# DeltaNet and GELU-MLP on one core: the norms' epsilon on Pool, one query mask by ScalarE and Pool, the last outputs from two queues, and a new order

## The chip, the cores and the metric

The kernel runs on one core of one Trainium2 chip. The time is the device time of one execution in microseconds, 270.38 us as the median of three runs. The engines are PE (TensorE, with its weight loads shown as PEld), DVE (VectorE), ACT (ScalarE), Pool (GpSimd) and SP (SyncE, which here only issues DMAs). Each engine works through its own queue in order and waits on semaphores for the others.

## The reference

`q`, `k` and `v` are (4, 8, 768, 48) and `beta` is (4, 8, 768), all f32. A delta rule runs over the 768 positions of each of the 32 heads, and a two-layer network with a GELU follows:

```python
k_n = k / (np.linalg.norm(k, axis=-1, keepdims=True) + 1e-06)
for t in range(S):
    y[:, :, t] = q[:, :, t] @ state                      # per head, state is 48 x 48
    v_old = k_n[:, :, t] @ state
    state = state + beta[:, :, t] * outer(k_n[:, :, t], v[:, :, t] - v_old)
x = y.transpose(0, 2, 1, 3).reshape(3072, 384)
h = x @ w_in                                             # 384 x 2048
g = 0.5 * h * (1 + tanh(sqrt(2 / pi) * (h + 0.044715 * h**3)))
out = g @ w_out                                          # 2048 x 384
```

The output is (3072, 384) in f32.

## The kernel before

The 768 positions are cut into 12 chunks of 64. A chunk has two units of eight head pairs each, so there are 24 units; unit `u` belongs to chunk `u // 2`. In each unit, 128 partitions hold two heads' 64 positions.

For each chunk, SP loads `k`, `q` and `v` (`k3.01` is one of four loads of chunk 3's keys). The norms are a short chain: `sq` (squares), `sum` (DVE), `pow` (the root; on ACT for the first two chunks, by a power on Pool after that), `eps` (adds 1e-6), `inv` (reciprocal) and `ib` (times minus beta). Chunk 0 is done in two halves, `0a` and `0b`. Minus beta comes from `betaT` (PE transposes) and `betaN` (eight small DVE copies).

For each unit, `kn` and `kb` scale the keys and `qb` converts the queries; `Tk`/`Tq` or `T` transpose them on PE and `kTk`/`kTq`/`kT` copy the result, or `turn` transposes by DMA. Products of keys with keys and queries (`GM` and `GQ` for units 0 to 3, `G2` and `G` for the rest) are copied through a triangular mask by DVE: `ln`, `wpm`, `wpq` or `wp`. A triangular system is then solved in five steps. `X1` sets up a block-diagonal tile `bd`; in step i a product `A` and a DVE addition `rt` (or, as an alternative, products `J` and `C` and a plain copy `rj`) give the right side of a product `B`, and B goes back into `bd`: either in two copies from PSUM (`bde`, ACT or DVE), or in one copy from PSUM (`xi`, ACT or DVE) and two from SBUF (`bdc`, Pool or DVE).

For each chunk, `K`, `R`, `U`, `Un`, `S`, `Sn` carry the state from chunk to chunk (`Sn` is the new state), and `Q`, `O`, `On` give the output `y`. `X` and `xT` transpose it on PE with a copy, or `turnx` by DMA. The network follows: 16 `up` groups of three matmuls, four `gelu` on ACT, eight `down` groups of four matmuls, two copies `Z` to SBUF, and the stores `out`. The `fill` operations are PE products of zeros.

What runs when is written out in one text, `ORDER`: a list of all operations with the engine behind a colon (`a` ACT, `d` DVE, `g` Pool, `s` SP) and the PSUM bank behind `@`. Each engine's queue is the list's operations on that engine, in the list's order. `Flow.add` names an operation with the engines that it may have, and what it reads and writes; `Flow.order` reads the text; `Flow.emit` works out the semaphore waits from the operations' reads and writes. Of two alternatives (`alt`), only the one named in the text runs.

The lines that the profile names: L333 is the helper `copy` (all plain copies); L416 the loads; L438 and L439 `sq`; L440 `sum`; L441 and L442 `pow`; L444 `eps`; L446 `inv`; L447 `ib`; L464 and L466 `kn` and `kb`; L475 `Tk`, `Tq`, `T`; L488 `turn`; L499 the products of keys and queries; L503 the masks; L529 and L531 `X1`; L540 `A`, `B`, `C`; L550 `rt`; L575 `bdc`; L397 and L402 `betaT` and `betaN`; L664 `X`; L681 `up`; L692 `down`; L701 and L704 the stores.

Of the kernel before, what the change touches and what calls it, by code (L numbers as in the profile page):

```python
# [29 lines left out]
Tq.1@0 fill37@6 J4.1@7 A5.0@3 fill19@6 X11.2:d ln.3 X10.2:d X11.3:d kTq.1:d wpm.3 w2.0 w2.1 C4.1 rj4.1:a sq.2:a bdz5:g X10.3:g R0b.0:g  # L30
A1.2@1 R0a.0:d rt5.0 C1.3 B4.1@0 bde40.1:a bde41.1:a GQ.1@6 B5.0@3 Tq.0@4 fill56@5 A5.1@0 rj1.3:d rt1.2 B1.2@5 rt5.1 sum.2 B5.1@2 kTq.0:d
wpq.1 fill65@0 B1.3@1 fill59@0 xi5.0:a bde11.2:a bde10.2:a bde50.1:a bde11.3:a bdc50.0:g bdc51.0:g qb.3:a bde51.1:a fill5@3 A2.2@0 bde10.3:d
A2.3@1 Tq.3@6 fill2@7 fill49@3 fill69@7 fill38@3 kTq.3:a rt2.2 rt2.3 B2.3@7 B2.2@6 bde20.2:a pow.2 eps.2 inv.2 bde20.3:d bde21.3:a bde21.2:d
U.0@2 GQ.0@0 GQ.3@4 Un.0:a A3.2@6 A3.3@7 qb.2:a wpq.0 rt3.3 O.0@2 fill6@0 B3.3@7 Tq.2@0 On.0:a X.0@1 wpq.3 rt3.2 xi3.3:a triwpm5:a S.0@2
fill28@7 kTq.2:d xT.0:d bdc31.3:d Sn.0:d B3.2@0 bde30.2:d bdc30.3:d kn.4:g ib.2:g kb.5:g bdz4:g kb.4:g kn.5:g sq.3:g qb.4:a qb.5:a bde31.2:a
ladj32.3:a up0.0@6 up1.0 up2.0 T.4@4 kT.4:d up3.0 up12.0@0 A4.2@2 A4.3@3 ladj16.3:d rt4.3 up13.0 G2.4@4 ladj16.2:a gelu0.0 up14.0 B4.3@3
rt4.2 ln.4 K.1@6 xi4.3:a up15.0 up4.0@4 up5.0 gelu3.0 R.1 bdc41.3:d sum.3 bdc40.3:g X10.4:g X11.4:g G.4@2 wp.4 B4.2@6 up8.0@0 up6.0 up7.0
up9.0 A5.3@7 up10.0 turn.5 q3.00 q3.01 q3.10 q3.11 k5.11 q4.00 k4.10 k5.00 k4.00 k5.10 q4.11 k4.01 k4.11 bde41.2:a bde40.2:a gelu1.0 rt5.3
A1.4@2 A5.2@3 GQ.2@6 G2.5@4 up11.0 rt1.4 rt5.2 wpq.2 B1.4@2 down10.0@3 pow.3 eps.3 inv.3 kn.6:g ln.5 kn.7:d ib.3:g kb.7:g X11.5:g X10.5:g
kb.6:g down11.0 B5.3@6 gelu2.0 bde11.4:a bde10.4:a G.5@0 Q.1@4 A2.4@2 B5.2@7 down12.0 down13.0 wp.5 rt2.4 bde50.2:d B2.4@2 down00.0@0  # L40
bde51.3:a qb.6:a qb.7:a bde51.2:a bde50.3:a A1.5@1 bde21.4:a rt1.5 U.1@6 turn.7 turn.6 k5.01 q6.11 bde20.4:a Un.1:a down01.0 B1.5@1 down02.0
O.1 A3.4@2 sq.4:d sum.4 pow.4 bde11.5:a bde10.5:a A2.5@1 down03.0 On.1:a Z1.0:a Z0.0:a rt3.4 rt2.5 X.1@4 B3.4@5 G2.7@2 bde31.4:a bde30.4:a
xT.1:d G.7@0 S.1@6 ln.7 Sn.1 B2.5@4 up8.1@2 A4.4@5 up9.1 bde20.5:a bde21.5:a sq.5:a eps.4 rt4.4 G2.6@6 up10.1 B4.4@5 A3.5@4 up11.1 ln.6
# [222 lines left out]
def bass_deltanet__then__act_gelu_tanh_kernel(  # L266
# [20 lines left out]
    A = F.add  # L287

    with nc.allow_non_contiguous_dma("strided loads"), nc.allow_low_precision("bf16 pipeline"):
# [39 lines left out]
        def hf(a, n=C):  # L329
            return slice(64 * a, 64 * a + n)  # L330

        def copy(e, out, in_):
            return e.activation(out, in_, ACT.Copy) if e is nc.scalar else e.tensor_copy(out, in_)  # L333

        PE, SP, EV = ("pe",), ("sp",), ("act", "dve")
        quad = [(p, a) for a in range(2) for p in range(2)]

# [418 lines left out]
```

## Time and profile before

| | |
|---|---|
| median of 3 runs (270.02 to 271.37) | 270.38 us |
| the profiled execution | 269.08 us |
| its span, first to last instruction | 267.4 us |
| mean granted TensorE clock | 0.997 |
| ACT busy | 191.3 us (72%) |
| Pool busy | 128.5 us (48%) |

The span is what the profile shows of the program; the execution's own time has 1.7 us more around it. The shares are of busy time, and for PE they say only that some matmul was under way. Sequencer work (waits, branches and issuing DMAs) does not count as busy. In a row of the timeline the first number is the start and the second the length, in microseconds from the start of the span.

### The profile page before, as it was taken

To read this page: it belongs to the slowest core of one execution; us is meant where nothing else is said; L and a number is where in the kernel's file an instruction comes from. 1 tells how busy PE (TensorE), PEld (TensorE's weight loads), DVE (VectorE), ACT (ScalarE), POOL (GpSimd) and SP (SyncE) were. 2 spreads that over 40 slices of the span, in tenths; PEclk is the share of its full clock that TensorE was granted. 3 is DMA by queue.
4 is the path that set the end of the run, shared out by engine and by line. 5 is a ranking of instruction groups with operands and counts; after the bars stand their busy time and mean duration, and the time that the engine had idled before them with its cause. 6 is when DMAs were issued, how large, how long until landed. Compare 5 with 4: busy or idle time off the path is not lost.

```text
span 267.4 us, 12235 instructions
## 1 busy us (share of the span) xinstructions
PE 242.7 (91%) x5476; PEld 188.9 (71%) x5484; DVE 212.3 (79%) x367; ACT 191.3 (72%) x298; POOL 128.5 (48%) x176
## 2 busy tenths in 40 slices
PE   1489768998999999999999999999999999999994
PEld 0266457776877787886877986976878868778672
DVE  4689999997899998898789987997898587786200
ACT  5646798689898878895887887784777837736450
POOL 5746556485788746671816532983652321011000
PEclk9999999999999999999999999999999999999998
DMA  4899997859889979899785979587515510331023
GB/s 79 143 169 187 163 193 122 151 109 141 170 144 159 145 136 169 160 153 133 158 166 92 178 136 133 103 173 130 87 44 100 99 32 2 93 61 29 5 60 88
DMA packets 119540, 32.05 MB, mean 120 GB/s; under 512 B 113600, under 2 KB 118720, under 8 KB 119488
## 3 DMA queue, kind: packets, MB, share of 16 engines
q1 hardware_dynamic: 115248, 27.88, 60.5%
q0 software_dynamic: 2880, 3.15, 7.4%
q8 instruction: 43, 0.70, 1.1%
q10 hardware_dynamic: 1360, 0.25, 0.5%
q14 instruction: 9, 0.07, 0.1%
HBM read 20.64 MB, written 4.72 MB: 95 GB/s over the span
## 4 chain that ended last, share of the span: by engine, by line
PE 55%; DVE 13%; ACT 11%; SPq 7%; DMA 6%; issue 2%; POOL 2%; ACTq 1%; DVEq 0%
PE ps L681 18%; PE ps L692 15%; PE ps L540 13%; SPq L416 6%; ACT bd L333 5%; DMA kT<-tok 4%; PE ps L499 3%; ACT gT L685 2%; DVE rt L550 2%; PE ps L606 2%; DVE bd L531 1%; DVE wp L503 1%; PE ps L652 1%; DVE bd L333 1%; DMA kraw<-in_k_dram 1%
## 5 line engine op out<-in xcount | busy, mean ns | idle before, releaser
L333 ACT ACTIVATE bd<-ps 64x512 bf16<-64x512 f32 x142 | 82.4, 589 | 23.6 <-PE ps L540 21.1
L681 PE MATMUL ps<-xT,W 128*128 128x256 bf16 x576 | 76.5, 273 | 0.6 <-ACT bd L333 0.4
L692 PE MATMUL ps<-W,gT 128*128 128x384 bf16 x384 | 73.3, 326 | 0.0
L685 ACT ACTIVATE gT<-ps 128x1024 bf16<-128x1024 f32 x48 | 48.4, 1020 | 13.9 <-PE ps L681 13.5
L681 PEld LDWEIGHTS ps<-xT,W 128*128 128x128 bf16 x576 | 50.5, 98 | 7.2 <-ACT bd L333 0.6
L550 DVE TENSOR_TENSOR rt<-ps,two 128x512 bf16<-128x512 f32 x67 | 45.2, 683 | 8.0 <-PE ps L540 7.5
L575 POOL COPY bd<-xi 64x256 f32<-64x256 f32 x39 | 16.5, 422 | 67.5 <-ACT xi L333 53.4
L692 PEld LDWEIGHTS ps<-W,gT 128*128 128x128 bf16 x384 | 33.1, 98 | 17.0 <-ACT gT L685 0.2
L529 POOL TENSOR_SCALAR_AFFINE_SELECT bd<-ln 64x512 bf16<-64x512 bf16 x35 | 23.1, 662 | 19.8 <-DVE ln L503 17.1
L442 POOL TENSOR_TENSOR nrm<-nrm,half 128x16 f32<-128x16 f32 x10 | 29.4, 2944 | 4.8 <-DVE nrm L440 4.1
L503 DVE CAST_PREDICATED wp<-mup,ps 128x1024 bf16<-128x1024 uint16 (+1 forms) x28 | 29.8, 1063 | 0.3
L540 PE MATMUL ps<-wp,bd 128*128 128x64 bf16 (+1 forms) x576 | 26.8, 188 | 3.2 <-ACT xi L333 0.9
L540 PE MATMUL ps<-rt,bd 128*128 128x64 bf16 x576 | 28.3, 194 | 0.9 <-DVE rt L550 0.7
L550 DVE TENSOR_TENSOR rl<-ps,two 128x256 bf16<-128x256 f32 (+1 forms) x47 | 22.4, 485 | 8.0 <-PE ps L540 7.7
L540 PEld LDWEIGHTS ps<-wp,bd 128*128 128x128 bf16 x576 | 22.7, 98 | 7.9 <-ACT bd L333 1.4
L333 DVE CAST bd<-ps 64x512 bf16<-64x512 f32 x38 | 25.9, 684 | 2.9 <-PE ps L540 2.3
L540 PEld LDWEIGHTS ps<-rt,bd 128*128 128x128 bf16 x576 | 23.5, 98 | 5.2 <-DVE rt L550 1.1
L540 PE MATMUL ps<-ln,bd 128*128 128x64 bf16 (+1 forms) x384 | 18.0, 188 | 2.8 <-DVE bd L333 1.6
L540 PEld LDWEIGHTS ps<-ln,bd 128*128 128x128 bf16 x384 | 14.9, 97 | 7.7 <-ACT bd L333 3.0
L503 DVE CAST_PREDICATED ln<-mlo,ps 128x512 bf16<-128x512 uint16 x24 | 16.4, 683 | 4.7 <-PE ps L499 4.4
L466 POOL TENSOR_TENSOR tok<-kraw,nrm 128x384 bf16<-128x384 f32 x22 | 18.1, 826 | 3.9 <-PE ps L639 3.3
L540 PE MATMUL ps<-rl,bd 128*128 128x64 bf16 x384 | 19.0, 193 | 0.7 <-DVE rl L550 0.7
(95 smaller groups left out, 324.0 us busy)
## 6 DMA issues: line engine op xcount, KB each, us to landing
qraw<-in_q_dram SPq DMA_DIRECT2D x48, 96.0 KB, 3.4
vraw<-in_v_dram SPq DMA_DIRECT2D x48, 96.0 KB, 3.5
kraw<-in_k_dram SPq DMA_DIRECT2D x44, 96.0 KB, 3.2
out_dram<-ob SPq DMA_DIRECT2D x22, 192.0 KB, 3.1
W<-in_moe_w_in_dram POOLq DMA_DIRECT2D x2, 768.0 KB, 10.4
W<-in_moe_w_out_dram POOLq DMA_DIRECT2D x2, 768.0 KB, 11.4
out_dram<-ob SPq DMA_DIRECT2D x4, 96.0 KB, 2.2
kT<-tok SPq DMA_TRANSPOSE x19, 4.6
```

The lines of the kernel that those rows point to most:

```text
L333: return e.activation(out, in_, ACT.Copy) if e is nc.scalar else e.tensor_copy(out, in_)
L416: lambda e, P, n=n, a=a, y=y, xs=xs, view=view: e.dma_start(raw[n][s][hf(a), :, :].rearrange("p (xg y) d -> p xg y d", y=2)[:, xs, y, :], ...
L442: if e is nc.scalar else e.tensor_tensor(nr[:, 1, hx], nr[:, 0, hx], half[:, hx], ALU.pow), reads=[nrn, "half"] + ["one"] * (c < ROOTS),
L466: A(("dve", "pool"), op("kb"), lambda e, P: e.tensor_tensor(kb, kr, nr[:, 4, hx].unsqueeze(2).to_broadcast(full), ALU.mult), reads=[f"kraw ...
L503: return e.copy_predicated(out.rearrange("p (x g) t -> p x g t", x=2), mask[:, 0:wd].bitcast(U16).unsqueeze(1).unsqueeze(1).to_broadcast([ ...
L529: A(("pool", "dve"), op(f"X1{a}"), lambda e, P, src=ln[m][hf(a), :, :], dst=bd[b_][hf(a), :, hf(a)], a=a: e.affine_select(out=dst, in_=src ...
L540: ins = e.matmul(P(name)[:, C * h + lo:C * h + C], bd[b_][:, h, :], rhs[:, h, lo:C], **kw)
L550: A(("dve",), op(f"rt{i}"), lambda e, P, i=i, lo=lo, r_=r_: e.tensor_tensor(r_[:, :, lo:C], P(ps(f"A{i}")).rearrange("p (h t) -> p h t", h ...
L575: A(("pool", "dve"), op(f"bdc{i}{a}"), lambda e, P, src=xi[i_][hf(a), :, :], dst=bd[b_][hf(a), :, hf(a)]: e.tensor_copy(dst.bitcast(F32), ...
L681: ins = e.matmul(P(ph)[:, 256 * f:256 * f + 256].rearrange("p (x t) -> p x t", x=2), W1[:, j, 128 * (i + f):128 * (i + f) + 128], x_[:, :, ...
L685: A(("act",), f"gelu{i // 4}.{c}", lambda e, P, i=i, ph=ph: e.activation(g_[:, i:i + 4, :], P(ph).rearrange("p (f t) -> p f t", f=4), ACT. ...
L692: ins = e.matmul(P(po)[:, 0:DM], g_[:, f, 128 * b:128 * b + 128], W2[:, f, :], start=(f == 0), stop=(f == FC - 1))
```

## The change

Four edits to what an operation may do, and a new `ORDER` for all of them:

- `eps` may run on Pool. In the new order 10 of the 13 do, each behind its `pow` in Pool's queue.
- The query mask of units 0 to 3 gets an alternative: `wqa`, a copy by ACT out of PSUM, and `wqb`, a product with the mask by Pool in SBUF, in place. The new order uses it for unit 1.
- The last chunk's four stores may be issued from SP or ACT, each with its own semaphore. In the new order `out01.11`, `out00.11` and `out10.11` are SP's and `out11.11` is ACT's.
- `betaN` goes through a helper `neg`, which knows ACT too; the engines allowed stay DVE alone.

```diff
+        def neg(e, out, in_):
+            return e.activation(out, in_, ACT.Copy, scale=-1.0) if e is nc.scalar else e.tensor_scalar(out, in_, -1.0, None, op0=ALU.mult)
...
-                A(("dve",), f"eps.{z}", lambda e, P, nr=nr, hx=hx: e.tensor_scalar(nr[:, 2, hx], nr[:, 1, hx], 1e-6, None, op0=ALU.add),
+                A(("dve", "pool"), f"eps.{z}", lambda e, P, nr=nr, hx=hx: e.tensor_scalar(nr[:, 2, hx], nr[:, 1, hx], 1e-6, None, op0=ALU.add),
...
+                A(("act",), op("wqa"), lambda e, P: copy(e, wp[s][:, :, C:2 * C].rearrange("p (x g) t -> p x g t", x=2), P(ps("GQ")).rearrange(
+                    "p (x r) -> p x r", x=2)[:, :, 0:4 * C].rearrange("p x (g t) -> p x g t", g=4)), frees=[ps("GQ")], writes=[n("wpq")], alt=(op("wq"), 1))
+                A(("pool",), op("wqb"), lambda e, P: e.tensor_tensor(wp[s][:, :, C:2 * C], wp[s][:, :, C:2 * C], mup[:, 0:C].unsqueeze(1).to_broadcast([128, H, C]), ALU.mult),
+                  reads=["mup"], writes=[n("wpq")], alt=(op("wq"), 1))
...
-                        A(SP, f"out{b}{a}.{c}", lambda e, P, a=a, b=b, r0=r0, o_=o_: e.dma_start(out[r0:r0 + C, :], o_[hf(a), b, :]), reads=[f"{on}.{b}"],
-                          dma=f"o{c % 2}")
+                        A(("sp", "act"), f"out{b}{a}.{c}", lambda e, P, a=a, b=b, r0=r0, o_=o_: e.dma_start(out[r0:r0 + C, :], o_[hf(a), b, :]),
+                          reads=[f"{on}.{b}"], dma=f"oz{b}{a}")
```

In the new order the counts of some operations on their engines differ as well (before, after):

| | DVE | ACT | Pool |
|---|---|---|---|
| `bde` | 38, 50 | 142, 132 | |
| `xi` | 6, 12 | 24, 17 | |
| `bdc` | 21, 16 | | 39, 42 |
| `X1` | 13, 9 | | 35, 39 |
| `eps` | 13, 3 | | 0, 10 |
| `qb` | 3, 2 | 12, 4 | 9, 18 |
| `sq` | 1, 1 | 5, 8 | 7, 4 |
| `xT` | 3, 0 | 1, 6 | |
| all | 367, 368 | 295, 274 | 168, 190 |

PE has 692 operations before and 689 after: 34 `fill` instead of 38, six `X` instead of four (chunks 7, 8 and 10 are turned by PE in place of DMA, chunk 6 by DMA in place of PE), and one `J` fewer. The text's beginning and end, before:

```
one:d tmplz:d tmpl0 tmpl1 pad1:d wz:g fill8@0 k0x0.00:a k0x0.01:a k0x0.10:s k0x0.11:s k0x1.10:a triln3:a k0x1.00:a half:d bdz1:d bdz3:d
...
down12.11 down13.11 down00.11@5 down01.11 down02.11 down03.11 out00.9 Z1.11:d out11.11 out10.11 out00.10 Z0.11:a out01.11 out00.11
```

and after, where ACT's queue begins with `k0x0.10 k0x0.11 k0x1.10 k0x1.11 k0x1.01 beta00 ladj16.3 two sq.0a tabS ladj32.0 pow.0a pow.0b` and the last words are

```
down02.11 down03.11 out00.10 Z0.11:d out01.11:s out00.11:s down12.11 down13.11 Z1.11:a out11.11:a out10.11:s
```

## The prediction

> **What bounds the kernel now.** I read the page's head first: the span, and each engine's busy time.
>
> ```profile
> span 267.4 us, 12235 instructions
> ...
> PE 242.7 (91%) x5476; PEld 188.9 (71%) x5484; DVE 212.3 (79%) x367; ACT 191.3 (72%) x298; POOL 128.5 (48%) x176
> ```
>
> PE is busy for 91% of the span, yet DVE and ACT are at 79% and 72%, and an average over the whole span hides which of them sets the pace where. So next came busy time by stage. I cut the stages at marks that exist in both orders: 17.6 us is where DVE starts `ln.1` (the second unit's first mask), 49.7 where it ends `kT.4` (chunk 2's first keys), 147.1 where it ends `rt4.13`, 241.2 where it ends `rt4.23` (the last unit's fourth step).
>
> ```profile
> 0.00:17.60 17.60, 7.73 (x105) 5.01 (x107) 10.90 (x38) 9.93 (x18) 10.81 (x26) 1.00 0.71 121
> ...
> 17.60:49.70 32.10, 25.97 (x555) 18.74 (x561) 30.05 (x53) 24.59 (x42) 18.39 (x22) 1.00 1.06 166
> 49.70:147.10 97.40, 93.81 (x2322) 73.92 (x2323) 86.91 (x140) 79.88 (x126) 61.09 (x70) 1.00 0.86 146
> 147.10:241.20 94.10, 92.79 (x2229) 74.81 (x2226) 78.48 (x130) 65.56 (x99) 37.70 (x57) 1.00 0.54 98
> 241.20:267.40 26.20, 22.36 (x274) 16.48 (x272) 5.99 (x11) 11.33 (x14) 0.52 (x1) 0.97 0.19 44
> ```
>
> The first number behind a window is its length; then come PE, PEld, DVE, ACT and POOL busy, each with its instructions. The opening is a start-up: PE has 7.73 of 17.6 us. From 17.6 to 49.7 DVE is full (30.05 of 32.1, 94%) while PE has 81%: DVE sets the pace. From 49.7 to 147.1 PE has 96% and DVE 89%: PE is the bound, and its gaps are opened by the engines that feed it. From 147.1 to 241.2 PE has 99% and DVE 83%: PE alone. The rest is PE's last feed-forward work and the outputs. So the span is a start-up, a stage paced by DVE, then PE's work plus its gaps, then a tail. A change of order is worth what it does to these four.
>
> The prices of the work that changes hands most, from the groups by line with shapes kept apart (busy, then mean ns of one, then idle time before):
>
> ```profile
> L333 ACT ACTIVATE bd<-ps 64x512 bf16<-64x512 f32 x142 | 82.4, 589 | 23.6 <-PE ps L540 21.1
> ...
> L333 DVE CAST bd<-ps 64x512 bf16<-64x512 f32 x38 | 25.9, 684 | 2.9 <-PE ps L540 2.3
> ...
> L333 DVE CAST xi<-ps 128x512 bf16<-128x512 f32 x6 | 4.1, 687 | 0.6 <-PE ps L540 0.5
> ...
> L575 DVE COPY bd<-xi 64x256 f32<-64x256 f32 x21 | 7.5, 359 | 1.4 <-ACT xi L333 0.9
> ...
> L444 DVE TENSOR_SCALAR nrm<-nrm 128x16 f32<-128x16 f32 x11 | 3.1, 286 | 0.5 <-POOL nrm L442 0.4
> ```
>
> **The change, part by part.** I counted the operations of both orders by name and engine and priced each by the mean of its own shape's group. Over the kernel DVE gets 12 more of the `bde` copies at 684 ns (+8.2) and 6 more `xi` (+4.1 at 687 ns), and gives away 10 epsilons (-2.9 at 286 ns), 5 `bdc` (-1.8 at 359 ns) and smaller things: all its operations come to 227.1 us before and 231.1 after. ACT loses 10 `bde` at 589 ns (-5.9) and others: 196.6 to 186.1. Pool gets 127.2 to 135.6. What counts is where these fall.
>
> *Start-up.* These rows of the timeline (start, length) are the chain from the first loads to the second unit's mask.
>
> ```profile
> 0.82 2.04 ACTq L416 DMA_DIRECT2D kraw<-in_k_dram  x3
> ...
> 2.89 1.28 ACT L333 ACT_TABLE_LOAD   x1 [2.89 <-issue]
> ...
> 4.72 0.51 ACT L438 ACTIVATE sq<-kraw 128x384 f32<-128x384 f32 x1
> ...
> 7.29 0.21 ACT L441 ACTIVATE nrm<-nrm 128x8 f32<-128x8 f32 x1
> ...
> 7.35 0.82 POOL L439 TENSOR_TENSOR sq<-kraw 128x384 f32<-128x384 f32 x1
> ...
> 7.53 0.68 DVE L444 TENSOR_SCALAR nrm<-nrm 128x8 f32<-128x8 f32 x1 [1.14 <-ACT nrm L441]
> ...
> 8.47 0.63 DVE L402 TENSOR_SCALAR bsb<-ps 64x8 f32<-64x8 f32 x4
> ...
> 9.18 0.57 POOL L447 TENSOR_TENSOR nrm<-nrm,bsb 128x8 f32<-128x8 f32 x1 [1.00 <-DVE bsb L402]
> ...
> 10.72 1.03 PE L475 MATMUL ps<-ident,tok 128*128 128x128 bf16 x8 [2.97 <-POOL tok L466]
> ...
> 13.44 1.37 PE L397 MATMUL ps<-identf,braw 32*128 32x32 f32 x11
> ...
> 16.89 0.64 PE L499 MATMUL ps<-kT 48*64 48x64 bf16 x32 [0.69 <-ACT kT L333]
> ...
> 17.59 0.69 DVE L503 CAST_PREDICATED ln<-mlo,ps 128x512 bf16<-128x512 uint16 x1
> ```
>
> Before, ACT issues three loads (0.68 us each, until 2.86), loads its table (until 4.17), squares at 4.72, has the root at 7.50, and PE transposes the first keys at 10.72. In the new order ACT issues six (five of `k0` and `beta00`) ahead of its first computation; behind them stand the table load, `ladj16.3`, `two` and the first square. Six times 0.68 from 0.82 on is 4.9, plus the table's 1.28 is 6.2, plus two short copies 6.6: the square comes 1.9 us later and ends at 7.1; a second table load of the same length and two short operations put the root's end at about 9.2 instead of 7.50. From the root to the transposes it took 3.2 us, in which the epsilon met Pool's square (0.68 us; 0.17 for the second one of this shape), four `betaN` took 0.63 and `ib.0a` on Pool 0.57. The new order has three `betaN` there, `ib.0a` on DVE (its other half took 0.26 there) and nothing of Pool's beside the epsilon: about 1.1 us less, so the transposes start at about 11.3 (+0.6). PE then has the 1.37 us of `betaT1` (row at 13.44) ahead of `GM.0`, where before it waited for the key copy and did `betaT1` afterwards; so `Tk.1` starts at about 14.75, as before, and `GM.1` (16.89) and `ln.1` (17.59) stay. I take 0, with ends of -0.7 (the table is loaded during the issues) and +1.9 (nothing is won back).
>
> *DVE's stage, to the end of `kT.4`.*
>
> ```profile
> 48.77 0.94 DVE L333 COPY kT<-ps 128x1536 bf16<-128x1536 bf16 x1
> ```
>
> From `ln.1` through this copy DVE's queue holds 52 operations before, 30.9 us by their means, which took 49.71 - 17.59 = 32.1 us: the means carry 1.04. The new order has 55 there, 31.5 us: two `bde`, two `xi`, two `rt` and a few presets more, two `bdc`, an `X1`, the state copy `Sn.0`, `xT.0` and `R0a.0` fewer. That is +0.6 us. At `G2.4`, which waits for this copy, PE has done six `up` groups of three matmuls before and four after, against one product of eight matmuls more. Two merged pieces of the chain that ended last give PE's price when it runs without a gap:
>
> ```profile
> 185.00 0.70 PE ps L540 x24
> ...
> 253.12 4.58 PE ps L681 x42
> ```
>
> 14 `up` groups in 4.58 us are 0.33 each, three products in 0.70 us 0.23 each: 0.65 less and 0.23 more of PE's work done. By this mark the new order is 0.6 + 0.65 - 0.23 = 1.0 us behind.
>
> *The long stage, to `rt4.13`.*
>
> ```profile
> 146.56 0.54 DVE L550 TENSOR_TENSOR rl<-ps,two 128x384 bf16<-128x384 f32 x1
> ```
>
> From `kT.4` on DVE has 139 operations and 93.6 us before, 133 and 91.8 after (five epsilons, two `qb`, an `Un`, an `xT` and a `sq` fewer; four `bdc`, two `bde`, two `xi` and two `kb` more). Counted from `ln.1` it is 124.5 against 123.3: 1.2 less. PE has the same 80 `up` and 40 `down` groups behind it at this point, and three products more (0.7 us). ACT's share of the stage falls from 85.6 to 81.2. If DVE sets the pace here, the new order reaches this mark 1.9 us ahead; if PE does, the 1.0 us behind stay. PE's share (96%) is nearer to full than DVE's (89%), but the gaps between the two are opened by DVE and ACT; I take the middle, -0.4, with the ends -1.9 and +1.0.
>
> *The last stage, to `rt4.23`.*
>
> ```profile
> 240.68 0.54 DVE L550 TENSOR_TENSOR rl<-ps,two 128x384 bf16<-128x384 f32 x1
> ```
>
> DVE has 129 operations and 84.1 us before, 130 and 87.0 after: eight `bde` more (+5.5), six `bdc` fewer (-2.2). PE has the same groups. In DVE's busy time that is 78.5 to 81.2 of 94.1 us, still 86%, so PE's queue covers most of it. If the cover fails the cost is all of the 2.9; I take +0.4, nearer to nothing as PE's row is at 99%.
>
> *The three named edits.* These rows price them (Pool's power and epsilon neighbours, the masks, the transposes).
>
> ```profile
> L442 POOL TENSOR_TENSOR nrm<-nrm,half 128x16 f32<-128x16 f32 x10 | 29.4, 2944 | 4.8 <-DVE nrm L440 4.1 <-DVE nrm L444 0.3
> ...
> L439 POOL TENSOR_TENSOR sq<-kraw 128x768 f32<-128x768 f32 x6 | 8.8, 1464 | 5.4 <-DMA kraw<-in_k_dram 5.4
> ...
> L503 DVE CAST_PREDICATED wp<-mup,ps 128x512 bf16<-128x512 uint16 x8 | 5.5, 685 | 0.1
> ...
> L447 POOL TENSOR_TENSOR nrm<-nrm,bsb 128x16 f32<-128x16 f32 x8 | 2.4, 296 | 0.4 <-DVE nrm L446 0.4
> ...
> L664 PE MATMUL ps<-ident,xo 128*128 128x128 bf16 x24 | 2.0, 220 | 0.1
> ```
>
> Epsilon on Pool: the nearest Pool row is the 128x16 product of L447, 296 ns; the bounds are DVE's 286 and the power's 2944 on the same shape. It stands in Pool's queue right behind the power, or one or two short operations later, so the result comes 0.3 us later, and `inv` on DVE waits for it; behind `inv` stand DVE's products. The power's 2.9 us leads that wait in both orders. Nothing on the path; DVE's saving is in the sums above.
>
> The query mask of unit 1: the DVE mask (685 ns) becomes an ACT copy `wqa.1`, near this row:
>
> ```profile
> L333 ACT ACTIVATE xi<-ps 128x512 bf16<-128x512 f32 x24 | 14.3, 595 | 6.3 <-PE ps L540 5.7 <-DVE bd L333 0.4
> ```
>
> and a Pool product `wqb.1` on 128x512, which no row shows; between that copy's length and 1464 ns (a Pool product of 768 f32), I take 1.1. Pool's queue holds `pow.2` (2.9), `eps.2`, `pad5` and `qb.3` ahead of it, some 4 us, and `O.0` on PE waits for it, with all of PE's queue behind. By the counts DVE ends `sum.2` 18.1 x 1.04 behind 17.6, near 36.4, so `wqb.1` ends near 41.6; `rt5.1` ends 21.4 x 1.04 behind, near 39.9, and by the copies that follow it (`bde50.1` and `bde51.1`, then `Un.0`) `O.0` is due near 42.7. So it is hidden by 1 us, and costs about as much if Pool is late by 2.
>
> Chunks 7, 8 and 10 are now turned by PE and chunk 6 by DMA, net two more on PE: 12 transposes at 2.0/24 = 83 ns are 1.0 us of PE's bound stage; I take 0.6, as they overlap their neighbours, between 0 and 1.0. SP's queue has two DMA transposes less.
>
> *The tail.*
>
> ```profile
> 263.65 0.49 ACT L333 ACTIVATE ob<-ps 128x384 f32<-128x384 f32 x1 [3.59 <-DMA out_dram<-ob]
> 264.17 1.11 SPq L701 DMA_DIRECT2D out_dram<-ob  x2
> ```
> ```profile
> L701 SPq DMA_DIRECT2D out_dram<-ob x4: 466/550/597, 261.6 to 264.7; - x4
> ...
> DMA to landing us min/median/max: 2.1/2.2/2.2
> ```
>
> PE's last result is copied by ACT at 263.65 to 264.14, and SP issues two stores one behind the other, 1.11 us; each lands 2.1 to 2.2 us after its issue. The new order issues one from SP and one from ACT, whose queue is empty then: the second issue's 0.55 us go, with the small hand-off 0.6. At least 0, at most 0.65.
>
> **The sum.** Start 0, opening and long stage together -0.4, last stage +0.4, transposes +0.6, tail -0.6: nothing is left on a span of 267.4 and a profiled run of 269.08. The median of the runs shown, 270.38, lies 1.3 above that run; on it I forecast 270.4.
>
> **A rule weighed.** This view gives the epsilon's least, median and greatest time.
>
> ```profile
> L444 DVE TENSOR_SCALAR nrm<-nrm x13: 165/172/1189, 7.5 to 194.4; 128x16 f32<-128x16 f32 x11, 128x8 f32<-128x8 f32 x2
> ```
>
> The least is 165 ns, and one epsilon took 1189. The one in the start-up's rows above took 680, while Pool squared beside it from 7.35 to 8.17. By means over least times, the 11 full epsilons cost (286 - 165) x 11 = 1.3 us more than they need; against Pool's 128.5 us that is a hundredth, and Pool's 8.4 us more would add 0.1. The Trainium skill, page "Advanced Engine Details and Errata", section "VectorE Performance Modes", says that VectorE's second port to SBUF is shared with GpSimd and that the two block each other. By it in full, each added Pool microsecond stops a DVE that is busy 79% of the time: an estimate of +6.6 us by that page. It speaks against giving Pool more; the row bears out the clash but a small price.
>
> **The rivals.** *DVE becomes the bound of the last stage (slower).* Place: 147 to 241 us; price: all of the 2.9 instead of 0.4, which gives 270.4 + 2.5 = 272.9. It decides from the point where DVE's busy share there passes some 95%, as in the opening. For it: 94% was enough to hold PE to 81% from 17.6 to 49.7. Against: PE's 99% and the lighter ACT.
>
> *DVE set the pace up to 147 (faster).* Then the -1.9 is had in full and the lighter ACT keeps the last stage at nothing: -1.9 + 0.6 - 0.6 = -1.9, so 268.5. For it: DVE's 94% and 89%. Against: PE's 96%.
>
> *The port (slower).* A DVE instruction on SBUF is stopped wherever one of Pool's added 8.4 us meets it, at DVE's 79%: +6.6, so 277.0. Against: the 1.3 us above, over the whole kernel.
>
> *The change doesn't do what it says (no change).* The two last stores share what moves them and land as before: 271.0. Or `O.0` waits 1 us for `wqb.1`: 271.4.
>
> **How the numbers follow.** About 0.5%, or 1.35 us, is what a measurement of this kernel can tell from no change. Forecast 270.4: 0.33. The two cases beside it, 0.04 each, also lie within 1.35: together 0.41. DVE in the last stage 0.29 and the port 0.03: slower 0.32. Faster 0.27. The forecast is the likeliest single case, and its own range is 269.1 to 271.7. The low end of the full range is the faster case with the transposes hidden (-0.6) and the start at its good end (-0.7): 267.2. The high end is DVE's case with the middle at its bad end (+1.0 instead of -0.4): 274.3. The port, and parts of the other cases' outer ends, lie beyond.
>
> **What would show it.** In the changed profile: the first square near 6.6 and the first PE transposes near 11.3; `ln.1` near 17.6; `kT.4` ending near 50.4; DVE busy near 81 us and PE 98% or more between `rt4.13` and `rt4.23`; the last two stores starting within 0.1 us of each other on SP's and ACT's queue. The forecast is wrong if `ln.1` starts after 19, if PE's busy share falls below 95% anywhere between 60 and 240 us, or if `rt4.13` ends before 145 or after 149.

## The result and the profile after

The changed kernel takes 272.06 us (median of 20 runs, 269.41 to 274.17); the kernel before, timed with it, 270.38 (20 runs, 267.59 to 274.33). The ratio is 1.0069, 95% interval 1.0043 to 1.0096: longer by 0.7% in this comparison. A second one, told below as run 2, gave 1.0017 (0.9987 to 1.0047): 271.94 against 271.94. The kernel before against itself, on another chip (run 1), came out at 1.0046 (0.9996 to 1.0096), so a half per cent is about the least that one comparison of twelve runs can tell. Whether the change costs anything is therefore not certain; if it does, it is less than one per cent. Ratios leave the most disturbed runs of each kernel out; medians hold all runs.

The page of the changed kernel, first lines:

```profile
span 271.7 us, 12247 instructions
...
PE 246.0 (91%) x5491; PEld 189.1 (70%) x5491; DVE 218.6 (80%) x368; ACT 181.5 (67%) x277; POOL 135.9 (50%) x198
...
PEclk9999979999999999999999999999999999999999
```

PE's share is as before, DVE has 80% instead of 79, ACT 67 instead of 72, Pool 50 instead of 48. One slice (the sixth, 34 to 41 us) has a granted clock of 0.7. Line numbers of the changed kernel are up to seven higher than before (`Tq` is L478 instead of L475). The stages are cut at the same four marks, which now stand at 18.04, 52.77, 152.52 and 245.31 us (columns as in the prediction):

```profile
0.00:18.04 18.04, 9.27 (x103) 5.15 (x104) 12.26 (x40) 7.25 (x14) 10.89 (x26) 1.00 0.74 127
18.04:52.77 34.73, 26.61 (x580) 18.64 (x577) 29.27 (x57) 23.33 (x38) 18.78 (x27) 0.95 0.98 155
52.77:152.52 99.75, 95.34 (x2361) 74.56 (x2361) 88.72 (x134) 76.38 (x118) 66.51 (x87) 1.00 0.89 144
152.52:245.31 92.79, 92.04 (x2148) 73.66 (x2147) 80.91 (x130) 64.33 (x96) 38.97 (x57) 1.00 0.48 88
245.31:271.70 26.39, 22.72 (x307) 17.09 (x304) 7.46 (x11) 10.21 (x12) 0.79 (x2) 0.99 0.22 53
```

The start-up is 0.4 us longer, the opening stage 2.6 (34.73 against 32.1), the long stage 2.4 (99.75 against 97.4), the last one 1.3 shorter (92.79 against 94.1), the tail 0.2 longer. One execution of each isn't enough, though: both kernels were profiled a second time in the runs below. With these, the ends of the marks are (us):

| mark | before | before again | after | after again |
|---|---|---|---|---|
| `kT.4` ends | 49.72 | 49.24 | 52.77 | 51.64 |
| `rt4.13` ends | 147.11 | 150.19 | 152.52 | 150.15 |
| `rt4.23` ends | 241.24 | 244.13 | 245.31 | 242.60 |
| span | 267.36 | 270.24 | 271.70 | 269.12 |

Up to `kT.4` the new order is 2.7 us later by the means of two. The long stage takes 97.4 and 101.0 before, 99.8 and 98.5 after: the two kernels can't be told apart there, since one kernel differs from itself by 3.6. The last stage is 1.4 shorter (94.0 to 92.6), the tail 0.3 longer. The sum is +1.6, near the 1.7 between the medians of the first comparison. By these four profiles the time is lost in the first 52 us, and some is won back behind 150; part of that last gain is only work that now stands elsewhere, as told below.

Within the opening stage, PE's row of the timeline has one wait in the midst of `Tq.0`, a group of four transposes (start, length, then the idle time before it and its releaser; "issue" means that nothing in the profile released it):

```profile
34.23 0.27 PE L478 MATMUL ps<-ident,tok 128*128 128x128 bf16 x2
36.17 0.37 PE L478 MATMUL ps<-ident,tok 128*128 128x128 bf16 x2 [1.67 <-issue]
```

Two transposes run, PE stands for 1.67 us, and the other two follow. No engine and no semaphore stands between them. The view of DMA queues, cut to stretches of time, shows what came late. Its rows give packets, MB and share of time. I take q8 for the queue that brings PE's instructions, its code: it moves 43 packets of 16 KB over the kernel, 0.70 MB, which over PE's 10982 instructions is 64 B each, or some 256 instructions a packet. From 21.5 to 33.5 us of the changed kernel:

```profile
q0 software_dynamic: 997, 0.98, 52.8%
q1 hardware_dynamic: 5021, 0.93, 51.6%
q14 instruction: 1, 0.01, 0.2%
```

From 33.5 to 36.2 us of it:

```profile
q0 software_dynamic: 521, 0.39, 92.0%
q1 hardware_dynamic: 522, 0.10, 33.7%
q8 instruction: 1, 0.02, 2.0%
```

And from 26 to 30 us of the kernel before:

```profile
q1 hardware_dynamic: 1686, 0.31, 52.3%
q0 software_dynamic: 302, 0.23, 51.3%
q8 instruction: 1, 0.02, 2.1%
```

q0 is the weights' queue, q1 the loads'. In the changed kernel q8 moved nothing from 21.5 to 33.5, while the loads and the second weight matrix (W2, the loads `w2`) filled the DMA engines: 52.8 and 51.6%. By the packets' own times PE's second fetch ran at 27.2 us in the old order, when PE had started 497 instructions, and at 33.9 in the new, when it had started 680. At 35.72, while PE still stands, the granted clock falls to a half for 3.41 us; I call such a stretch a halved window. Three equal windows, the halved one last:

```profile
28.90:32.31 3.41, 2.74 (x99) 1.73 (x95) 3.24 (x7) 2.60 (x5) 0.13 (x1) 1.00 1.12 152
32.31:35.72 3.41, 1.90 (x44) 1.23 (x45) 3.24 (x6) 3.19 (x6) 2.51 (x4) 1.00 1.27 185
35.72:39.13 3.41, 2.96 (x45) 2.41 (x44) 1.17 (x4) 1.01 (x2) 1.79 (x3) 0.50 1.28 185
```

PE is busy for 1.90 of 3.41 us in the second; in the third the clock is 0.50, and DVE, which waits for PE, is busy for 1.17. The Trainium skill, page "TensorE: Matmul & The Clock Gate", section "Part 1: The HAM clock gate (the "warmup" mystery)", says that PE's clock is halved by windows of 3413 ns after one that was idle. The trace agrees in the length (3.41) and the half; but a window with 56% of work was enough here.

### The profile page after: what moved, and what is told of

Same layout as the page of the kernel before. It is cut to its first block, busy times and chain, and to the rows that moved or that the text cites. A ratio compares the mean times of both kernels' runs of the same rounds, so it can differ in the third digit from the quotient of the medians.

```text
span 271.7 us, 12247 instructions
## 1 busy us (share of the span) xinstructions
PE 246.0 (91%) x5491; PEld 189.1 (70%) x5491; DVE 218.6 (80%) x368; ACT 181.5 (67%) x277; POOL 135.9 (50%) x198
## 4 chain that ended last, share of the span: by engine, by line
PE 64%; DVE 19%; ACT 4%; DMA 4%; SPq 3%; issue 2%; ACTq 1%; POOL 1%; DVEq 0%
PE ps L688 19%; PE ps L699 18%; PE ps L547 15%; DVE bd L333 3%; PE ps L502 3%; DVE rt L557 3%; PE ps L613 2%; DMA kraw<-in_k_dram 2%; DVE wp L506 2%; DMA vraw<-in_v_dram 2%; ACT bd L333 2%; SPq L419 2%; DVE bd L582 1%; PE ps L634 1%; ACTq L419 1%
## 5 line engine op out<-in xcount | busy, mean ns | idle before, releaser
L333 ACT ACTIVATE bd<-ps 64x512 bf16<-64x512 f32 x132 | 76.6, 589 | 22.6 <-PE ps L547 20.2
L688 PE MATMUL ps<-xT,W 128*128 128x256 bf16 x576 | 78.4, 273 | 0.0
L557 DVE TENSOR_TENSOR rt<-ps,two 128x512 bf16<-128x512 f32 x68 | 45.8, 683 | 6.6 <-PE ps L547 5.9
L536 POOL TENSOR_SCALAR_AFFINE_SELECT bd<-ln 64x512 bf16<-64x512 bf16 x39 | 26.3, 676 | 32.2 <-DVE ln L506 23.5
L333 DVE CAST bd<-ps 64x512 bf16<-64x512 f32 x50 | 33.9, 686 | 4.6 <-PE ps L547 3.6
L506 DVE CAST_PREDICATED wp<-mup,ps 128x1024 bf16<-128x1024 uint16 (+1 forms) x27 | 29.1, 1077 | 2.7 <-PE ps L502 2.5
L547 PE MATMUL ps<-wp,bd 128*128 128x64 bf16 (+1 forms) x576 | 27.2, 189 | 2.4 <-DVE rl L557 0.8
L469 POOL TENSOR_TENSOR tok<-kraw,nrm 128x384 bf16<-128x384 f32 x20 | 17.0, 856 | 12.4 <-PE ps L646 7.0
L547 PE MATMUL ps<-ln,bd 128*128 128x48 bf16 (+1 forms) x384 | 18.3, 188 | 2.1 <-DVE bd L333 1.1
L547 PEld LDWEIGHTS ps<-rl,bd 128*128 128x128 bf16 x384 | 16.1, 99 | 4.2 <-DVE rl L557 1.0
```

The source lines that it names most:

```text
L469: A(("dve", "pool"), op("kb"), lambda e, P: e.tensor_tensor(kb, kr, nr[:, 4, hx].unsqueeze(2).to_broadcast(full), ALU.mult), reads=[f"kraw ...
L506: return e.copy_predicated(out.rearrange("p (x g) t -> p x g t", x=2), mask[:, 0:wd].bitcast(U16).unsqueeze(1).unsqueeze(1).to_broadcast([ ...
L536: A(("pool", "dve"), op(f"X1{a}"), lambda e, P, src=ln[m][hf(a), :, :], dst=bd[b_][hf(a), :, hf(a)], a=a: e.affine_select(out=dst, in_=src ...
L547: ins = e.matmul(P(name)[:, C * h + lo:C * h + C], bd[b_][:, h, :], rhs[:, h, lo:C], **kw)
L557: A(("dve",), op(f"rt{i}"), lambda e, P, i=i, lo=lo, r_=r_: e.tensor_tensor(r_[:, :, lo:C], P(ps(f"A{i}")).rearrange("p (h t) -> p h t", h ...
L688: ins = e.matmul(P(ph)[:, 256 * f:256 * f + 256].rearrange("p (x t) -> p x t", x=2), W1[:, j, 128 * (i + f):128 * (i + f) + 128], x_[:, :, ...
```

## The experiments

The theory: in the new order PE's second code fetch (counted from the kernel's start) comes late behind W2's load, PE stands, the clock halves, and these make the loss. Rivals: the opening's own order is slower; DVE's additional work costs in the last stage; the named edits cost. All ratios are to the kernel before, run beside them. Runs 1, 9, 10 and 3 shared one chip, 2, 8, 5 and 6 a second, 7, 4, 11 and 12 a third; before had medians of 271.93, 271.94 and 272.02 there. In all, the end of `G2.4` is the mark of the opening: 50.11 in the prediction's profile of before, 53.23 in that of after. `rt1.6` is a later mark: 75.2 and 75.4 in the two profiles of before, 78.9 and 77.8 in those of after. Each run's kernel has its own line numbers (the helper `copy`, L333 so far, is L322, L326 or L327 in the runs).

**1. The kernel before again** (no edit).

> The kernel before once more, unchanged, as the measure of what two equal kernels differ by, and for the granted clock of each of its runs. Every theory: ratio 1.000 within 0.003. Code-fetch theory (PE in the new order runs out of code at 34.5 us because a fetch of its instructions comes late among the loads, and its clock is then halved for 3.4 us): in this kernel most runs have a mean granted clock of 0.997 or more, against 0.993 or 0.994 in 12 of 20 runs of the changed kernel, and no halved clock between 20 and 60 us in the profile. Rival (the clock has nothing to do with the order): as many runs at 0.994 here.

271.99 against 271.93 us, ratio 1.0046 (0.9996 to 1.0096); `G2.4` at 49.79, the clock whole between 20 and 60. But against the expectation 8 of its 12 runs had a mean clock under 0.9965, and 47 of the 87 runs of before beside all twelve, against 22 of 32 of the changed kernel: the halved windows are the old order's too, hardly less often. The time goes with them: among the first 20 runs of the changed kernel the six at 0.997 or more average 270.87 us, the ten at 0.993 or 0.994 (one halved window) that the ratio counts 271.97, 1.1 us more. And this profile's long stage was 3.6 us longer than the first one's with the clock whole. Its two longest waits of PE there, which are 0.9 and 0.6 in the first profile, in the view of waits from 49.2 to 150.2 us (total, times, longest):

```profile
PE ps L540 <- ACT xi L333: 1.5, 1, 1.5
PE ps L499 <- DMA kT<-tok: 1.2, 1, 1.2
```

**2. The changed kernel again** (no edit).

> The changed kernel once more, unchanged, beside the three that follow, for a second profile of it and the granted clock of its runs. Up to 33 us its profile repeats the first to 0.1 us (keys' transposes, masks, products). Code-fetch theory: PE's second code fetch is served after 32 us again, and PE stands for 0.5 to 1.7 us near 34.5; the clock is halved in some runs and not in others (a mean of 0.994 stands for one halved window of 3.41 us). Ratio 1.003 to 1.010. Rival (the stall was a chance of one profile): fetch by 30 us and no gap, and the ratio as before, so that the loss lies in the order itself.

271.94 us, ratio 1.0017 (0.9987 to 1.0047). The fetch ran at 34.1, and PE stood at the same two transposes:

```profile
36.33 0.27 PE L478 MATMUL ps<-ident,tok 128*128 128x128 bf16 x2 [1.94 <-issue]
```

This time the clock stayed whole, though the window behind (34.67 to 38.08) had PE busy for 1.75 us only; `G2.4` ended at 52.11 instead of 53.23. So the stall belongs to the order, and the halved clock is a chance on top, 1.1 us at this mark by these two profiles. The wait came in every profile that keeps this opening and W2's place in it: 1.67, 1.94, 1.94, 2.26 and 1.99 us behind PE's 695th instruction (after, after again, and the runs 5, 6 and 7 below), and 1.12 behind the 691st (run 10). Three of these six had a halved window beside it (after, runs 5 and 6).

**3. W2 later.** One edit in the order of the changed kernel:

```diff
- bdc20.0:g ... w2.0 w2.1 ... bdc41.1:g bdc40.1:g
+ bdc20.0:g ... bdc41.1:g bdc40.1:g w2.0 w2.1
```

> The changed kernel with one edit: the load of the second weight matrix is issued by Pool some 13 us later, behind bdc40.1 (about 40 us instead of 26.7). Code-fetch theory: fewer transfers stand ahead of PE's second code fetch, so it is served by 31 us instead of 33.9, the 1.67 us gap near 34.5 is under 0.5, the clock stays whole, and the ratio against the kernel before falls from 1.007 to 0.997-1.002. Rival (the opening's own order, its waits for keys, copies and masks, is slower): gap or not, ratio 1.005 to 1.009. If the first down-projection near 60 us waits for the weights, the ratio rises by what it waits.

The fetch ran at 31.6, PE's wait without a cause was gone, and the clock stayed whole. Yet `G2.4` ended at 52.41, and the time is 271.98 us, ratio 1.0031 (0.9997 to 1.0066), above the expected 0.997 to 1.002. The two issues took 1.94 us of Pool's queue right ahead of `pow.2`, so that `eps.2`, `inv.2` and `wpq.0` came late, and PE waited 1.65 us for that mask at 42.9:

```profile
44.51 0.38 PE L471 MATMUL ps<-ident,tok 128*128 128x128 bf16 x4 [1.65 <-DVE wp L499]
```

The stall was exchanged for a wait.

**4. W2 later still, in two halves**, where no power stands behind it:

```diff
- ... w2.0 w2.1 ... wqb.1 ... qb.5:g
+ ... wqb.1 w2.0 ... qb.5:g w2.1
```

> The changed kernel with the second weight matrix's two loads issued by Pool behind wqb.1 and qb.5 (some 44 and 49 us) instead of 26.7, where they also delay no power. Code-fetch theory: second fetch served by 32 us, no wait of PE without a cause near 34.5, G2.4 ends by 51.0 (52.1 to 53.2 in the changed kernel), median 270 to 271.3, fewer runs with a halved clock. Rival (the stall hides behind DVE's and ACT's chain): G2.4 at 52 or later, median as the changed kernel's.

The opening did what the theory says: fetch at 31.4, no wait near 34.5, `G2.4` at 51.06, 1.05 ahead of the changed kernel where its clock was whole (run 2). But the kernel took 278.70 us (six runs, 274.77 to 280.43), ratio 1.0211 (1.0122 to 1.0300). PE's waits from 50 to 62 us:

```profile
PE ps L495 <- DMA kT<-tok: 2.5, 1, 2.5
PE ps L540 <- issue: 2.2, 1, 2.2
```

W2's 1.5 MB now moved from 44 to 60 us and met the loads and a key transpose of SP's, which took 12.7 us from issue to landing, against a median of 4.3 in the changed kernel:

```profile
kT<-tok SPq DMA_TRANSPOSE x1, 12.7
```

Later PE waited 3.0 us more for another key transpose. Of the 2.2 us without a cause I can't say that it was code: the fetch had ended 3.8 us before PE went on, against 1.3 to 1.7 in the others. The expected total, 270 to 271.3, was wrong by 7 to 9 us. W2 no longer collides with the code, but with what moves at its new place.

**5. The mask of unit 1 back on DVE.**

```diff
- bde11.3:a wqa.1 bde51.0:a ... qb.2:d rt2.2 ... wpq.0 wqb.1
+ bde11.3:a bde51.0:a ... qb.2:d wpq.1 rt2.2 ... wpq.0
```

> The changed kernel with unit 1's query mask given back to DVE (0.69 us, put where DVE waited 1.2 us for PE near 42 us); the ACT copy wqa.1 and Pool's product are gone. Theory that the named mask edit costs time: wqa.1's 0.60 us stands in ACT's queue between bde11.3 and bde51.0 on the chain that ended last, so rt2.2's wait and G2.4 come 0.4 to 0.6 us earlier and the ratio is 0.002 lower than the changed kernel's in the same job. Rival (hidden, as predicted): G2.4 within 0.2 us of the changed kernel's where the clock and the code fetch behave alike, same ratio.

271.74 us, ratio 1.0030 (0.9997 to 1.0063); `G2.4` at 53.10 with one halved window, against 53.23 in the changed kernel with one. DVE took the mask in a gap, as its timeline shows:

```profile
41.42 0.34 DVE L326 CAST tok<-qraw 128x384 bf16<-128x384 f32 x1
41.68 0.68 DVE L499 CAST_PREDICATED wp<-mup,ps 128x512 bf16<-128x512 uint16 x1
42.62 0.69 DVE L550 TENSOR_TENSOR rt<-ps,two 128x512 bf16<-128x512 f32 x1 [0.26 <-PE ps L540]
```

No cost and no gain of the mask edit shows.

**6. Every epsilon on DVE, at the same places.**

```diff
- eps.1:g ... eps.11:g
+ eps.1:d ... eps.11:d
```

> The changed kernel with every epsilon of the norms on DVE again, at the same places of the order. Predicted: nothing on the path, so the ratio equals the changed kernel's within 0.002. Rival (epsilon on Pool is late for the reciprocal): the DVE waits for Pool's epsilon (0.4 to 0.6 us each where they occur) are replaced by waits for Pool's power as long, ratio 0.001 to 0.003 lower. Port rule in the small: DVE's 286 ns each, 2.6 us in all, come back as PE gaps in the last stage: ratio 0.002 to 0.005 higher.

278.47 us, ratio 1.0279 (1.0225 to 1.0333): the largest effect of all, and neither my forecast nor a rival had it in this size. DVE and Pool from 43.5 to 45.6 us:

```profile
43.50 0.25 POOL L361 MEMSET tok<- 128x192 f32 x1
43.57 1.77 DVE L440 TENSOR_SCALAR nrm<-nrm 128x16 f32<-128x16 f32 x1 [1.77 <-POOL nrm L438]
43.71 0.49 POOL L326 CAST tok<-qraw 128x384 bf16<-128x384 f32 x1
44.17 1.14 POOL L512 TENSOR_TENSOR wp<-wp,mup 128x512 bf16<-128x512 bf16 x1
45.26 0.35 DVE L326 CAST tok<-qraw 128x384 bf16<-128x384 f32 x1
```

L438 is `pow` here, L440 `eps`. In the new order `eps` stands directly or closely behind `pow`. (For two of the ten, `eps.0b` and `eps.1`, the root is ACT's, not Pool's.) On DVE, `eps.2` holds DVE's queue until Pool's power of 2.9 us is done (1.77 us of idling), and then itself takes 1.77 us while three Pool instructions run: `G2.4` ended at 56.65, with two halved windows up to 51 us. Over the kernel DVE waits for the power three times, 4.1 us:

```profile
DVE nrm L440 <- POOL nrm L438: 4.1, 3, 1.8
```

Three epsilons ran long as well (1.77, 0.44 and 0.46 us instead of 0.17). Together these are 6.3 us of DVE's time, near the 6.5 between this run and the changed kernel on the same chip; how much each of them, and the halved windows, put into the total is not shown. On Pool the epsilon holds nobody: only `inv`, later, waits.

**7. Every epsilon on DVE, directly ahead of its reciprocal.**

```diff
- pow.2 ... eps.2:g ... inv.2
+ pow.2 ... eps.2:d inv.2
```

> The changed kernel with the ten epsilons on DVE again, now each directly ahead of its reciprocal in the order instead of directly behind the power. Theory from the run with them behind the power (6.5 us slower): DVE's queue stood still for Pool's power there, and the price of an epsilon on DVE is only its 0.29 us where it stands late. So the time comes back to the changed kernel's: median 271.5 to 273, DVE's waits for Pool's power under 1 us in all. Rival (DVE has no room for the epsilons in this order): 274 or more.

273.57 us, ratio 1.0097 (1.0055 to 1.0139), between the two expectations; no wait of DVE for Pool's power is left, and the median epsilon takes 169 ns. The changed kernel had 1.0069 in its first comparison and 1.0017 in its second, on other chips: against the one that is 0.3% and within the intervals, against the other 0.8%. One profile doesn't show where the time would go (`G2.4` at 52.65, 0.5 late). So nearly all of run 6's loss came from the place of the epsilons; whether one on Pool is worth anything against a well placed one on DVE stays open.

**8. The old start-up, to some 25 us, then the new order.**

```diff
- bdz1:g k0x0.10:a bdz2:d ... Tk.3@1 ... qb.1:g
+ one:d tmplz:d tmpl0 ... Tk.3@2 ... kTk.3:d bdz2:g qb.1:d
  bdz4:d ladj16.3:a triln2:g J4.0@2 ... rj2.1:d Tq.1@6 B2.1@0 ...
```

> The old order up to the third unit's key copy (its start-up and the stage to some 25 us), then the new order with its fills. If the loss is made before 25 us, where PE in the new order waits four times for 0.6 to 1.05 us between 19.9 and 25.8: rt1.6 ends by 76.5 and the ratio is 0.998 to 1.002. If it is made between 25 and 50 us (the code fetch, ACT's and DVE's chain near 40): rt1.6 after 77 and ratio 1.004 to 1.009.

271.75 us, ratio 1.0003 (0.9960 to 1.0045); `rt1.6` at 77.83, `G2.4` at 52.16, PE's wait without a cause 0.73 us at 35.0 (behind its 693rd instruction), and one halved window, from 30.5 to 33.9, ahead of that wait. By the mark the loss lies behind 25 us; the ratio can't tell.

**9. The old opening, then the new order**, cut ahead of the first feed-forward group:

```diff
- bdz1:g k0x0.10:a bdz2:d ... B3.3@5 Sn.0:a bde31.3:a
+ one:d tmplz:d tmpl0 ... bde31.2:a ladj32.3:a ladj16.3:a ladj16.2:d GQ.2@0 wpq.2
  up12.0@6 A4.2@4 up13.0 up14.0 rt4.2 ...
```

> The old order up to the last operation ahead of the first feed-forward group, then the new order. Loss made in the opening (my theory): ratio 0.997 to 1.001, G2.4 ends near 52 (it has one query gram and its mask more behind it than the old one), no halved clock before 60 us. Loss made by DVE's 2.9 us more in the last stage (rival): ratio 1.006 to 1.009.

271.23 us, ratio 0.9989 (0.9945 to 1.0033). `G2.4` ended at 52.07, as expected, for two reasons. One is the seam, the place where I joined the two orders: `GQ.2`, a product of chunk 1's queries that the old order has later, held PE for 1.7 us at 45.4. The other is a halved window from 47.9 to 51.3, though none had been expected before 60. Behind this the new order's last stage and tail ran as in the changed kernel.

**10. The new opening, then the old order.**

```diff
- one:d tmplz:d tmpl0 ... bde31.2:a ladj32.3:a
+ bdz1:g k0x0.10:a bdz2:d ... B3.3@5 Sn.0:a v2.11 xi3.3:a bdc31.3:d bdc30.3:d sq.3:g
  up0.0@6 up1.0 up2.0 T.4@4 kT.4:d ...
```

> The new order up to the last operation ahead of the first feed-forward group, then the old order. Loss made in the opening: ratio 1.005 to 1.010, PE without work for 1 us or more near 34 to 36 us, clock halved once for 3.4 us. Loss made later (rival): ratio 0.999 to 1.002.

275.79 us (twelve runs, 271.36 to 278.87), ratio 1.0105 (1.0041 to 1.0169), with PE's wait of 1.12 us at 34.4 and `G2.4` at 52.4: the loss of the opening, and nothing won back behind it. The halved window fell at 86 us, not near 36.

**11. The old order with W2 earlier**, to make the old order's fetch late:

```diff
- qb.0:g ... bdc10.1:g ... w2.0 w2.1
+ qb.0:g w2.0 w2.1 ... bdc10.1:g
```

> The kernel before with one edit: the second weight matrix's loads issued behind qb.0 (some 22 us) instead of 26, so that they stand ahead of PE's second code fetch, which was served at 27.2 and 28.5. Code-fetch theory: that fetch is served after 31 us, PE stands 0.5 to 2 us without a cause near 32 to 35, G2.4 ends 1 to 2 us later (51 to 52), ratio 1.003 to 1.010. Rival (a fetch this late costs the old order nothing): fetch late but no wait of PE, ratio 0.998 to 1.003.

273.70 us, ratio 1.0120 (1.0060 to 1.0179), but not by my mechanism. Pool's timeline (the wait before a row, and its releaser, in brackets):

```profile
20.96 0.83 POOL L322 CAST tok<-qraw 128x384 bf16<-128x384 f32 x1
26.55 1.82 POOL L416 DMA_DIRECT2D W<-in_moe_w_out_dram  x2 [4.76 <-DMA vraw<-in_v_dram]
28.36 0.42 POOL L564 COPY bd<-xi 64x256 f32<-64x256 f32 x1
```

The issue waits for chunk 0's `v`: the program has `w2` read `vraw00` and `vraw01`, so that W2 doesn't start before those loads have landed, the last of them at 26.27. So the edit could not bring W2 forward: it went out at 26.55, where the old order has it at 25.98, half a microsecond behind the same landing (25.43). What the edit did was to hold Pool's queue for 4.76 us, and PE waited 3.3 us for `bdc10.1` behind it. The fetch ran at 33.3, but PE, held by `bdc10.1` and by a halved window from 30.3 to 33.7, had started only 601 instructions by then and didn't run out of code. That a late fetch alone would stall the old order is not shown.

**12. The old opening and the new order, seam mended**, against run 9:

```diff
- ladj16.2:d GQ.2@0 wpq.2 up12.0@6 ... bde51.3:a bde50.3:a
+ ladj16.2:d up12.0@6 ... bde51.3:a GQ.2@2 wpq.2 bde50.3:a
```

> The old opening and the new order behind it, with the query gram that held PE for 1.7 us at the seam moved behind bde51.3. Opening theory (the new order is worse up to 50 us and better behind it): G2.4 ends near 50, median 268.5 to 270.5, ratio 0.990 to 0.997, below both kernels. Rival (the gain behind 50 us in the old opening's hybrid was chance): median 271 to 272.5.

`G2.4` ended at 50.04, as expected; the kernel took 272.07 us, ratio 1.0043 (1.0003 to 1.0083), as the rival had it. The 2 us won in the opening were lost again behind it in this profile, `rt1.6` at 78.92 (a halved window from 65.3 to 68.8 is part of it). PE's waits from 62 to 160 us:

```profile
PE ps L541 <- DVE rt L551: 2.0, 1, 2.0
PE ps L682 <- DMA xT<-xo: 1.9, 1, 1.9
```

So no version here beats both kernels by what these comparisons can tell. The runs show why PE stands near 34.5 us and that W2's place decides it; they don't show that the stall makes the difference in the total. Without it the ratio was 1.0031 (run 3, with another wait in its place), with it 1.0069 and 1.0017.

## Why the prediction was right or wrong

The forecast was 270.4, no difference. The 272.06 us lie 0.4 above its own range (269.1 to 271.7) and within the full one (267.2 to 274.3). Against the kernel before it is +1.7 us in the first comparison, a little beyond the 1.35 that I had called too small to tell, and nothing in the second. So "no difference" came about as nearly as these runs can say. That the sum came to nothing was partly luck: steps failed in both directions.

**The base.** The two profiles of before differ by 2.9 us in span and by 3.6 in the long stage alone. I worked the sum against one, a short one, and moved it by 1.3 to the median; the spread of one stage between executions was no term of mine, and it is larger than every term.

**Start-up: right.** The first square started at 6.53 (forecast 6.6), the transposes at 11.38 (11.3), `ln.1` at 18.04 (17.6): 0.4 late. Its product `GM.1` was ready at 17.51; two presets (`bdz5`, `ladj32.1`) stood ahead of `ln.1` in DVE's queue, and I had followed PE's queue alone.

**The opening: the mechanism failed.** I held that DVE sets the pace there, 52 to 55 operations, and that `G2.4` would be 1.0 behind. DVE was busy for 29.27 of 34.73 us, 84%: it waited for PE. With the code wait taken away (run 4) the mark was 51.06, 1.1 behind the 50.0 of the old orders, near the forecast's 1.0, but not for its reason, since DVE didn't set the pace. With the wait it is 52.11, with the halved clock 53.1 to 53.2. The failing step is that PE's waits were counted only from what other engines release; a late instruction fetch and the clock aren't in any count of operations.

**The long stage: not tested as finely as it was forecast.** I took -0.4 for opening and stage; `rt4.13` ended at 152.5 and 150.2, both past the 149 that I had named as the mark of a wrong forecast, but the kernel before was at 150.2 too when profiled again. One bound of that term doesn't add up either: DVE's queue was 1.2 us shorter by my own count, and the 1.9 seems to add the 0.7 of three PE products to it. With 1.2 the middle is -0.1 instead of -0.4, and the sum 270.7.

**The last stage: sign wrong, rival refuted.** +0.4 became -1.4. DVE was busy for 80.91 us (forecast 81) and PE for 99% (98 or more), so DVE's 2.9 us more cost nothing that shows. I had counted the same groups for PE; but counted by their ends within the two marks, two `K`, two `A`, one `B` and one `up` fewer and two `X` more stand there. PE's busy time is 0.75 us less (92.79 to 92.04), in the second profiles 0.9 (92.89 to 91.97). That is work which now stands ahead of this stage or behind it, and no gain. What is left is 0.6 us less of PE standing, in both pairs of profiles.

**The transposes (+0.6): open.** Group `X` has 36 matmuls and 3.0 us instead of 24 and 2.0; no run took it alone.

**The tail: mis-sized.** The two last stores were issued as forecast, within 0.1 us of each other (the last of SP's three at 268.59 too):

```profile
267.36 1.78 SPq L708 DMA_DIRECT2D out_dram<-ob  x3
268.07 0.49 ACT L333 ACTIVATE ob<-ps 128x384 f32<-128x384 f32 x1 [3.53 <-PE ps L699]
268.59 0.55 ACTq L708 DMA_DIRECT2D out_dram<-ob  x1
```

```profile
out_dram<-ob SPq DMA_DIRECT2D x3, 96.0 KB, 2.2
out_dram<-ob ACTq DMA_DIRECT2D x1, 96.0 KB, 2.5
```

From the last copy's end to the end of the span it takes 3.22, 3.21 and 3.25 us with four stores on SP (before, before again, run 10), and 3.14, 3.28, 3.41 and 3.14 with one on ACT (after, after again, runs 9 and 3). The last packet moves 0.2 us earlier (2.13 to 2.19 behind the copy against 2.40), but the end of the span follows it by 1.0 to 1.3 us instead of 0.8; why is not shown. The 0.6 was 0: the rival "they land as before" was right.

**Epsilon on Pool: the price right, the point missed.** The rows of the changed kernel:

```profile
L447 POOL TENSOR_SCALAR nrm<-nrm 128x16 f32<-128x16 f32 x9 | 2.8, 314 | 0.8
L449 DVE RECIPROCAL nrm<-nrm 128x16 f32<-128x16 f32 x11 | 2.7, 244 | 0.4 <-POOL nrm L447 0.4
```

314 ns (forecast 296), and 0.4 us of waiting in all (0.8 in the second profile). What I didn't see is that Pool's epsilon also keeps DVE's queue free of the wait for Pool's power: 6.5 us at these places (run 6). A late epsilon on DVE avoids that wait too (run 7).

**The mask: right, with both ends late.** `wqb.1` took 1.16 us (forecast 1.1) and ended at 45.27, 1.2 ahead of `O.0`, which started at 46.47 (forecast 1.0); run 5 confirms it. But both came later than the forecast times, 41.6 and 42.7, by 3.7 and 3.8 us. `sum.2` ended at 35.84, near the forecast 36.4, yet `pow.2` started only at 40.08: `bdc41.1` stood ahead of it in Pool's queue and waited until 39.25 for DVE's `xi`. That the distance between the two was kept is in part luck.

**The port rule.** As a price for the whole kernel (+6.6) it is refuted by the measured 1.7. But run 6 shows the clash at one instruction: 1.77 us for an epsilon that takes 0.17 alone, ended with the third Pool instruction. The Trainium skill, page "Advanced Engine Details and Errata", section "VectorE Performance Modes", says that GpSimd's instructions and VectorE's 2p instructions (those with two read ports) block each other. This row fits it if the epsilon is such an instruction, which no run shows; my estimate had taken the rule for every VectorE instruction.

## What to carry to other kernels

Ask of an operation that waits for a slow engine not what it takes but whose queue it holds: ten epsilons of 0.2 to 0.3 us cost 6.5 us in DVE's queue behind a slow power, and in Pool's hardly anything. Before a change of order is summed by operations, profile the kernel twice; a stage that differs from itself by more than the terms can't be summed that finely. And look whether a large load stands ahead of an engine's code: moving the load by some microseconds took the stall away here, and what it meets instead has to be looked for. Before a load is moved, look what its issue waits for: run 11 moved only the wait.

## What had not been expected of the hardware

PE's code comes in packets of 16 KB, some 256 instructions, on a queue of its own beside the data's, and PE stood for 0.73 to 2.26 us without any semaphore in all seven profiles in which a fetch came 5 to 7 us later than in the old order and PE had come to some 690 instructions before that fetch was done. The Trainium skill, page "Runtime: NRT & Kernel Launch", section "Instruction fetch mechanics", calls the cost of crossing such a 16 KB block mostly hidden; here it was not while the DMA engines were full (a share of 1.27 from 32.31 to 35.72 us). One halved window of 3.41 us goes with 1.1 us in the run's time. Such windows came behind the stall in three profiles, but also where there was none (run 9) and ahead of it (run 8), so the stall is not their only cause.
